# A fused SwiGLU feed-forward kernel: all loads issued by SyncE, ScalarE's table load first, x tile 1 transposed ahead of gate 0

## The chip, the cores and the metric

The kernel runs on one core of a Trainium2 chip. The time is the device time of one execution in microseconds; the figure compared is the median over runs. Five engines work side by side: TensorE (PE for matmuls, PEld for the load of their stationary operand), VectorE (DVE), ScalarE (ACT), GpSimd (POOL) and SyncE (SP). SyncE and ScalarE issue DMAs here, each on a queue of its own, and the same 16 DMA engines move the data of both.

## The reference

```python
def reference(x, w_gate, w_up, w_down):
    g = _silu(x @ w_gate)
    u = x @ w_up
    return (g * u) @ w_down
```

x is 1 x 2048 x 512, w_gate and w_up are 512 x 1376, w_down is 1376 x 512, all bf16.

## The kernel before

The 2048 tokens are worked in four chunks of 512. TensorE multiplies with 128 rows of the contraction at a time, so x must lie transposed: `xT_sb` holds it as 4 blocks of 128 features by 2048 tokens. For each chunk and each 128 columns of the weights there are a gate group and an up group, each of 4 matmuls into one of 8 PSUM banks; ScalarE applies silu to the gate bank, VectorE multiplies that by the up bank into `hT_sb`. The last 96 columns are worked apart (groups X and Y). Then comes the product with w_down, in strips, and the copies to `o_sb`, which SyncE (one of them ScalarE) stores.

The order on every queue is written out by hand, and semaphores tie the engines together. What concerns the change is the first chunk, where work starts before most of the input is there:

- Loads. ScalarE issues the first gate slab (128 columns, `load_gate(act, *slabs[0])`, line 121) and x tile 1 (line 122), then comes its table load for silu with a dummy activation (line 277). SyncE issues x tile 0, up slab 0, gate and up slabs of 1 and 2 column blocks, then two DMA transposes (`x0b`, `x0c`: tokens 256 to 383 and 384 to 511, line 95), the remaining gate and up slabs, the other chunks of x by DMA transpose, and w_down. A slab is named by its first block of 128 columns: `wg0`, `wu0`, `wg1`, `wu1`, `wg2`, `wu2`, `wg4`, `wu4` and so on.
- x tiles 0 and 1 (128 tokens each) are loaded as they lie (`load_xn`, line 115) and transposed by TensorE (`transposes`, line 367, four matmuls of 128 x 128 against an identity); VectorE and ScalarE copy the four results in turns from PSUM to `xT_sb` (lines 302 and 288).
- TensorE (`on_tensor`) starts with matmuls on constants (`warm`, line 358) that give no result, five of 512 columns and two of 128. Then, in this order: transposes of tile 0, two more such matmuls (`N_GAP`), gate group 0 on the first 128 tokens (four matmuls), transposes of tile 1, up group 0 on the first 128 tokens, both groups on tokens 128 to 255, the other six groups of the first eight banks on tokens 0 to 255, the first two groups on tokens 256 to 383 (they need `x0b`) and 384 to 511 (`x0c`), the other six on 256 to 511, and from there on whole groups of 512 tokens (line 326 throughout), the next of which needs `wg4`.

`need(name)` makes TensorE wait for a load, `after(engine, n)` for the n-th result of VectorE or ScalarE.

Of the kernel before, what the change touches and what calls it, by code (L numbers as in the profile page):

```python
# [14 lines left out]
def bass_standalone__swiglu_ffn__prompt_kernel(nc, x, w_gate, w_up, w_down, out):  # L15
    _, S, D = x.shape
    F = w_gate.shape[1]
    P = 128
# [32 lines left out]
    with ExitStack() as es:  # L51
# [33 lines left out]
        def load_sem(name):  # L85
            loads[name] = sem(f"s_{name}")
            return loads[name]
# [6 lines left out]
        def load_x(eng, name, t0, t1):  # L94
            eng.dma_start_transpose(
                xT_sb[:, :, t0:t1], xf[t0:t1, :]
            ).then_inc(load_sem(name), 16)

        def load_w(eng, name, src, base, f0, f1):
            eng.dma_start(  # L100
                w_sb[:, :, base + f0:base + f1],
                src[:, f0:f1].rearrange("(k p) f -> p k f", p=P),
            ).then_inc(load_sem(name), 16)

        slabs = [(0, 1), (1, 2), (2, 4), (4, 7), (7, NFT)]
        slab_of = {ft: a for a, b in slabs for ft in range(a, b)}

        def load_gate(eng, a, b):
            load_w(eng, f"wg{a}", w_gate, 0, a * P, min(b * P, F))

        def load_up(eng, a, b):
            load_w(eng, f"wu{a}", w_up, UPH, a * P, min(b * P, F - 32))

        def load_xn(eng, i):
            eng.dma_start(xn_sb[:, i, :], xf[i * P:(i + 1) * P, :]).then_inc(load_sem(f"xn{i}"), 16)
# [1 line left out]
        def out_rows(t):  # L117
            return of[t * P:(t + 1) * P, :]

        def loads_on_scalar(act):  # L120
            load_gate(act, *slabs[0])
            load_xn(act, 1)

        def loads_on_sync(sp):
            load_xn(sp, 0)
            load_up(sp, *slabs[0])
            for a, b in slabs[1:3]:
                load_gate(sp, a, b)
                load_up(sp, a, b)
            load_x(sp, "x0b", HT, HT + P)  # L130
            load_x(sp, "x0c", HT + P, SC)
            for a, b in slabs[3:]:
                load_gate(sp, a, b)
                load_up(sp, a, b)
            load_w(sp, "wut", w_up, F - (F - 32), F - 32, F)
            for c in range(1, NSC):
                load_x(sp, f"x{c}", c * SC, (c + 1) * SC)
            sp.dma_start(
                wd_sb[:, 0:NFF, :], w_down[0:NFF * P, :].rearrange("(k p) d -> p k d", p=P)
            ).then_inc(load_sem("wd"), 16)  # L140
            load_sem("wdt")
            for y0 in (0, 64):
                sp.dma_start(wd_sb[y0:y0 + 64, T01, :], w_down[NFF * P:F - SR, :]).then_inc(loads["wdt"], 16)
            for x0 in range(0, P, SR):
                sp.dma_start(wd_sb[x0:x0 + SR, T2, :], w_down[F - SR:F, :]).then_inc(loads["wdt"], 16)
            sp.dma_start(wd_sb[0:F_LAST, TAIL, :], w_down[NFF * P:F, :]).then_inc(load_sem("wdl"), 16)
# [7 lines left out]
        def add_group(kind, **what):  # L154
            g = dict(kind=kind, at=len(groups), bank=banks[len(groups) % NB], readers=[], **what)
            groups.append(g)
            return g
# [76 lines left out]
        for at, t in enumerate(tiles):  # L234
# [3 lines left out]
            for c0, c1 in parts:  # L238
                g = add_group("O", t=t, c0=c0, c1=c1)
                eng = "A" if at % 2 == 1 and c0 == 0 else "D"  # L240
                op = add_op(
                    eng, g, kind="copy", out=o_sb[ob][:, c0:c1], src=g["bank"][:, 0:c1 - c0],
# [8 lines left out]
        def ready(op):  # L251
            return op["ready"] if "ready" in op else (s_P, op["g"]["at"] + 1)

        def store_tiles(eng, own):
            for o, t, c0, c1, ob, copied, n in stores:
                if o == own:
                    eng.wait_ge(s_A if copied == "A" else s_D, n)
                    eng.dma_start(out_rows(t)[:, c0:c1], o_sb[ob][:, c0:c1]).then_inc(s_out[ob], 16)

        def on_sync(sp):  # L260
            loads_on_sync(sp)
            store_tiles(sp, "S")
            for i in range(NOS):
                sp.wait_ge(s_out[i], 16 * n_store[i])
# [8 lines left out]
            pool.tensor_copy(hl_sb[64:96, :], hx_sb[64:96, c, SC - P:SC]).then_inc(s_L, 1)  # L273

        def on_scalar(act):
            loads_on_scalar(act)
            act.activation(adummy[:, 0:4], zero_c, ACT.Silu)  # L277
            for op in act_ops:
                act.wait_ge(*ready(op))
                if op["kind"] == "silu":  # L280
                    if op["free"]:
                        act.wait_ge(s_D, op["free"])
                    fn = ACT.Silu
                else:
                    if op["stored"][1]:
                        act.wait_ge(*op["stored"])
                    fn = ACT.Copy
                act.activation(op["out"], op["src"], fn).then_inc(s_A, 1)  # L288
            store_tiles(act, "A")
# [15 lines left out]
        def on_tensor(pe):  # L305
# [25 lines left out]
            def gu_needs(g, n0, n1):  # L331
                c, ft = g["c"], g["ft"]
                if c > 0:
                    need(f"x{c}")
                if c == 0 and n1 > HT:
                    need("x0b")
                if c == 0 and n1 > HT + P:
                    need("x0c")
                need(("wg" if g["kind"] == "G" else "wu") + str(slab_of[ft]))

            def gu_step(g, dk, n0, n1):
                c = g["c"]
                col = (0 if g["kind"] == "G" else UPH) + g["ft"] * P
                if c == 0:
                    for i in range(n0 // P, min(n1 // P, NXN)):
                        after(*xt_ready[i, dk])
                ins = whole(g["bank"], dk, col, c, n0, n1)
                if n1 == SC and dk == KD - 1:
                    ins.then_inc(s_P, 1)

            def gu_matmuls(g, n0, n1):
                gu_needs(g, n0, n1)
                for dk in range(KD):
                    gu_step(g, dk, n0, n1)

            def warm(n, width):
                for i in range(n):
                    pe.matmul(banks[NB - 1][:, 0:width], lhsT=ones_w, rhs=ones_m[:, 0:width], start=True, stop=True)  # L358
# [5 lines left out]
            def transposes(i):  # L364
                need(f"xn{i}")
                for dk in range(KD):
                    pe.matmul(  # L367
                        tview(i, dk), lhsT=xn_sb[:, i, dk * P:(dk + 1) * P], rhs=ident[:, :],
                        start=True, stop=True, is_transpose=True,
                    ).then_inc(s_X, 1)  # L370

            first = groups[0:NB]
            transposes(0)
            warm(N_GAP, P)
            gu_matmuls(first[0], 0, P)
            transposes(1)
            gu_matmuls(first[1], 0, P)
            for dk in range(KD):
                for g in first[0:2]:
                    gu_step(g, dk, P, HT)  # L380
# [108 lines left out]
        on_sync(nc.sync)  # L489
        on_gpsimd(nc.gpsimd)  # L490
        on_scalar(nc.scalar)
        on_tensor(nc.tensor)
        on_vector(nc.vector)

# [27 lines left out]
```

## Time and profile before

| | us |
|---|---|
| median of 3 runs (lowest, highest) | 120.07 (120.05, 120.31) |
| the profiled execution | 120.41 |
| its span, first to last instruction | 119.1 |
| TensorE busy (matmul) | 116.5 |
| VectorE, ScalarE busy | 38.3, 35.2 |

The queues, from the page (packets, MB, share of the 16 engines' time over the span): q1 is SyncE's, q10 ScalarE's.

```profile
q1 hardware_dynamic: 16816, 8.33, 27.5%
q10 hardware_dynamic: 816, 0.36, 1.1%
```

A line of the timeline reads: start in us, length in us, engine, line of the kernel, operation, output<-inputs, shape, and how many like instructions in a row it merges; in brackets, the idle time of the engine before it and what ended it. SPq and ACTq are the issue of a DMA by SyncE and ScalarE, whose length is that of the issue and not of the transfer. The view of DMAs gives for each issue the KB and the us from its start to the landing of the last byte. A matmul's length in the trace includes its way through the array, which overlaps with the next one; the rate is seen from start to start.

### The profile page before, as it was taken

What the parts mean: (1) busy time and instruction counts of PE and PEld (TensorE: products, weight loads), DVE (VectorE), ACT (ScalarE), POOL (GpSimd) and SP (SyncE); (2) the same over time, 40 slices, a digit from 0 to 9 for tenths busy, and PEclk for the clock granted to TensorE, in tenths of its full rate; (3) what the DMA queues carried; (4) which work ended last, traced back from release to release, by engine and by line L of the source; (5) the groups of instructions that cost most, each with busy time, mean ns of one, the idle gap of its engine ahead of it and who ended that gap; (6) DMA issues with size and microseconds to landing.
All of it is one profiled execution on the core that took longest, in us unless ns stands there. A gap on an engine that the chain in (4) does not pass through costs nothing.

```text
span 119.1 us, 2344 instructions
## 1 busy us (share of the span) xinstructions
PE 116.5 (98%) x1019; PEld 60.6 (51%) x1019; DVE 38.3 (32%) x61; ACT 35.2 (30%) x62; POOL 1.0 (1%) x7
## 2 busy tenths in 40 slices
PE   7999999999999999999999999999999999999993
PEld 2899544444444444444444444444444445885452
DVE  0204633444334444334453344361000044003321
ACT  3406444262343272442353432430000033003021
POOL 1000000000000000000000000001000000000000
DMA  4999989991000000000000000000000017200612
GB/s 84 296 176 347 265 178 239 265 340 29 0 6 0 0 0 0 0 6 0 0 0 6 0 0 0 0 0 6 0 6 0 0 51 235 77 0 6 204 61 88
DMA packets 17642, 8.83 MB, mean 74 GB/s; under 512 B 10624, under 2 KB 17632, under 8 KB 17632
## 3 DMA queue, kind: packets, MB, share of 16 engines
q1 hardware_dynamic: 16816, 8.33, 27.5%
q10 hardware_dynamic: 816, 0.36, 1.1%
q8 instruction: 8, 0.13, 0.4%
q14 instruction: 2, 0.02, 0.1%
HBM read 4.75 MB, written 2.10 MB: 58 GB/s over the span
## 4 chain that ended last, share of the span: by engine, by line
PE 98%; DVE 0%; issue 0%
PE bank L326 62%; PE bank L444 25%; PE bank L483 7%; PE bank L358 2%; PE bank L406 2%; PE bank L367 1%; DVE o_sb L302 0%
## 5 line engine op out<-in xcount | busy, mean ns | idle before, releaser
L326 PE MATMUL bank<-xT_sb,w_sb 128*128 128x512 bf16 (+2 forms) x384 | 73.7, 356 | 0.0
L326 PEld LDWEIGHTS bank<-xT_sb,w_sb 128*128 128x128 bf16 x384 | 37.0, 100 | 36.3
L298 DVE TENSOR_TENSOR hT_sb<-sg_sb,bank 128x512 bf16<-128x512 f32 x40 | 27.5, 687 | 40.5 <-PE bank L326 39.6
L288 ACT ACTIVATE sg_sb<-bank 128x512 f32<-128x512 f32 x40 | 23.8, 596 | 40.9 <-PE bank L326 40.8
L444 PE MATMUL bank<-wd_sb,hT_sb 32*128 32x512 bf16 x496 | 29.0, 374 | 0.0
L444 PEld LDWEIGHTS bank<-wd_sb,hT_sb 32*128 32x128 bf16 x496 | 15.2, 93 | 11.6 <-issue 0.4
L302 DVE CAST o_sb<-bank 128x512 bf16<-128x512 f32 (+1 forms) x10 | 5.7, 595 | 31.1 <-PE bank L444 25.9
L288 ACT ACTIVATE o_sb<-bank 128x512 bf16<-128x512 f32 (+1 forms) x8 | 4.3, 582 | 33.6 <-PE bank L444 27.9
L483 PE MATMUL bank<-wd_sb,hT_sb 128*128 128x512 bf16 (+2 forms) x56 | 8.1, 304 | 0.0
L483 PEld LDWEIGHTS bank<-wd_sb,hT_sb 128*128 128x128 bf16 x56 | 4.2, 97 | 4.2 <-issue 0.4
L444 PE MATMUL bank<-wd_sb,hy_sb 32*128 32x512 bf16 (+1 forms) x32 | 5.0, 371 | 0.0
L298 DVE TENSOR_TENSOR hx_sb<-sgx_sb,bank 32x512 bf16<-32x512 f32 x4 | 2.8, 692 | 3.5 <-ACT sgx_sb L288 3.5
L288 ACT ACTIVATE sgx_sb<-bank 32x512 f32<-32x512 f32 x4 | 2.3, 587 | 4.5 <-PE bank L326 4.5
L358 PE MATMUL bank<-const-bfloat16-1.0 128*128 128x512 bf16 (+1 forms) x9 | 2.9, 486 | 0.8 <-PEq L507 0.8
L444 PE MATMUL bank<-wd_sb,hx_sb 32*128 32x512 bf16 (+1 forms) x16 | 3.0, 371 | 0.0
L288 ACT ACTIVATE sgy_sb<-bank 64x512 f32<-64x512 f32 x4 | 2.4, 590 | 0.1
L358 PEld LDWEIGHTS bank<-const-bfloat16-1.0 128*128 128x128 bf16 x9 | 1.1, 140 | 2.1 <-issue 2.1
L406 PE MATMUL bank<-xT_sb,w_sb 128*64 128x512 bf16 x16 | 1.9, 382 | 0.0
L444 PEld LDWEIGHTS bank<-wd_sb,hy_sb 32*128 32x128 bf16 x32 | 1.6, 93 | 0.6
L302 DVE COPY xT_sb<-bank 128x128 bf16<-128x128 bf16 x4 | 0.9, 224 | 3.0 <-PE bank L367 3.0
L277 ACT ACT_TABLE_LOAD x1 | 1.3, 1283 | 1.8 <-issue 1.8
L406 PEld LDWEIGHTS bank<-xT_sb,w_sb 128*64 128x64 bf16 x16 | 0.8, 109 | 1.0 <-DVE hT_sb L298 0.4
(16 smaller groups left out, 7.3 us busy)
## 6 DMA issues: line engine op xcount, KB each, us to landing
out_dram<-o_sb SPq DMA_DIRECT2D x15, 128.0 KB, 1.8
wd_sb<-in_w_down_dram SPq DMA_DIRECT2D x1, 1280.0 KB, 8.3
w_sb<-in_w_gate_dram SPq DMA_DIRECT2D x1, 480.0 KB, 5.5
w_sb<-in_w_up_dram SPq DMA_DIRECT2D x1, 448.0 KB, 7.5
w_sb<-in_w_gate_dram SPq DMA_DIRECT2D x1, 384.0 KB, 4.0
w_sb<-in_w_up_dram SPq DMA_DIRECT2D x1, 384.0 KB, 4.4
w_sb<-in_w_up_dram SPq DMA_DIRECT2D x2, 128.0 KB, 3.3
w_sb<-in_w_gate_dram SPq DMA_DIRECT2D x1, 256.0 KB, 3.7
```

What stands on the lines that cost most here:

```text
L277: act.activation(adummy[:, 0:4], zero_c, ACT.Silu)
L288: act.activation(op["out"], op["src"], fn).then_inc(s_A, 1)
L298: ins = dve.tensor_tensor(op["out"], op["a"], op["b"], ALU.mult)
L302: ins = dve.tensor_copy(op["out"], op["src"])
L326: return pe.matmul(bank[:, n0:n1], lhsT=w_sb[:, dk, col:col + P], rhs=xT_sb[:, dk, c * SC + n0:c * SC + n1], start=(dk == 0), stop=(dk == ...
L358: pe.matmul(banks[NB - 1][:, 0:width], lhsT=ones_w, rhs=ones_m[:, 0:width], start=True, stop=True)
L367: pe.matmul(tview(i, dk), lhsT=xn_sb[:, i, dk * P:(dk + 1) * P], rhs=ident[:, :], start=True, stop=True, is_transpose=True,).then_inc(s_X, 1)
L406: ins = pe.matmul(g["bank"][y0:y1, :], lhsT=w_sb[:, dk, YC0:YC0 + 64], rhs=xT_sb[:, dk, c * SC:(c + 1) * SC], start=(dk == 0), stop=(dk == ...
L444: ins = pe.matmul(g["bank"][:, 0:c1 - c0], lhsT=h, rhs=wd_sb[r0:r0 + SR, w, c0:c1], start=(start and fk == fks[0]), stop=(stop and fk == f ...
L483: ins = pe.matmul(g["bank"][:, 0:c1 - c0], lhsT=h, rhs=w, start=(last and fk == 0), stop=(fk == (NFF if last else NFF - 1)), skip_group_ch ...
```

## The change

SyncE takes over ScalarE's two loads: its order becomes x tile 0, gate 0, x tile 1, up 0, and from there as before. ScalarE's first instruction is then the table load. On TensorE the transposes of tile 1 come directly after the two filler matmuls, ahead of gate group 0, and the gate and up groups on the first 128 tokens follow one after the other.

```diff
-        def loads_on_scalar(act):
-            load_gate(act, *slabs[0])
-            load_xn(act, 1)
-
         def loads_on_sync(sp):
             load_xn(sp, 0)
+            load_gate(sp, *slabs[0])
+            load_xn(sp, 1)
             load_up(sp, *slabs[0])
             for a, b in slabs[1:3]:
                 load_gate(sp, a, b)
...
         def on_scalar(act):
-            loads_on_scalar(act)
             act.activation(adummy[:, 0:4], zero_c, ACT.Silu)
...
             transposes(0)
             warm(N_GAP, P)
-            gu_matmuls(first[0], 0, P)
             transposes(1)
-            gu_matmuls(first[1], 0, P)
+            for g in first[0:2]:
+                gu_matmuls(g, 0, P)
             for dk in range(KD):
                 for g in first[0:2]:
                     gu_step(g, dk, P, HT)
```

## The prediction

> **What bounds the kernel now.** I read the page's busy times and chain first, then the order of time of the first 16 us, then the landings, then the traffic in stretches.
>
> ```profile
> PE 116.5 (98%) x1019; PEld 60.6 (51%) x1019; DVE 38.3 (32%) x61; ACT 35.2 (30%) x62; POOL 1.0 (1%) x7
> ...
> PE 98%; DVE 0%; issue 0%
> ```
>
> TensorE is busy or in line for 98% of the span and the chain that ends last lies on it throughout. So a change to loads can move the time only through TensorE's few waits, all in the first 10 us, through the clock it starts with, or through the last stores. In order of time:
>
> ```profile
> 0.74 0.46 ACTq L100 DMA_DIRECT2D w_sb<-in_w_gate_dram  x1
> 0.74 0.40 SPq L115 DMA_DIRECT2D xn_sb<-in_x_dram  x1
> ...
> 1.19 0.42 SPq L100 DMA_DIRECT2D w_sb<-in_w_up_dram  x1
> 1.23 0.53 ACTq L115 DMA_DIRECT2D xn_sb<-in_x_dram  x1
> ...
> 1.79 1.28 ACT L277 ACT_TABLE_LOAD   x1 [1.79 <-issue]
> ...
> 3.26 0.35 PEld L367 LDWEIGHTS bank<-ident,xn_sb 128*128 128x128 bf16 x4 [0.25 <-issue]
> 3.29 0.58 PE L367 MATMUL bank<-ident,xn_sb 128*128 128x128 bf16 x4
> ...
> 3.67 0.42 PE L358 MATMUL bank<-const-bfloat16-1.0 128*128 128x128 bf16 x2
> 3.70 0.49 ACT L288 ACTIVATE xT_sb<-bank 128x128 bf16<-128x128 bf16 x2 [0.41 <-PE bank L367]
> ...
> 3.96 0.58 PE L326 MATMUL bank<-xT_sb,w_sb 128*128 128x128 bf16 x4
> ...
> 4.41 0.61 PE L367 MATMUL bank<-ident,xn_sb 128*128 128x128 bf16 x4
> ```
>
> The transposes of tile 0 start at 3.29 because x tile 0 lands then; the warm-up matmuls stopped at 3.07 (the last of them starts at 2.97 and passes on after 0.107), so 0.22 us are idle. After the two filler matmuls (done at 3.88) the gate matmuls wait 0.08 for the copies of tile 0; after them the transposes of tile 1 wait 0.05 for x tile 1. From 4.81 on no matmul waits. The landings, from each issue:
>
> ```profile
> w_sb<-in_w_gate_dram ACTq DMA_DIRECT2D x1, 128.0 KB, 2.9
> xn_sb<-in_x_dram SPq DMA_DIRECT2D x1, 128.0 KB, 2.4
> xn_sb<-in_x_dram ACTq DMA_DIRECT2D x1, 128.0 KB, 3.1
> ```
>
> So gate 0 lands at 3.59, x tile 0 at 3.15, x tile 1 at 4.36. The granted clock is 1.00 in every row, yet matmuls of one shape have two rates:
>
> ```profile
> 4.91 1.17 PE L326 MATMUL bank<-xT_sb,w_sb 128*128 128x128 bf16 x9
> ...
> 8.74 0.94 PE L326 MATMUL bank<-xT_sb,w_sb 128*128 128x128 bf16 x14
> ```
>
> Leaving out the last one's own duration (0.31 and 0.22 us, the rows of single instructions): (1.17-0.31)/8 = 0.107 us each early, (0.94-0.22)/13 = 0.056 later. The step comes at 5.95. Time lost before it therefore holds up work that could be made good at the double rate, if the step stays at 5.95: such a loss costs 1 - 0.056/0.107 = 0.48 of itself.
>
> ```profile
> 1.75:2.25 0.50, 0.50 (x3) 0.15 (x1) 0.00 (x0) 0.46 (x1) 0.00 (x0) 1.00 0.94 113
> 2.25:3.07 0.82, 0.82 (x4) 0.30 (x2) 0.00 (x0) 0.82 (x1) 0.00 (x0) 1.00 1.10 268
> 3.07:3.29 0.22, 0.21 (x2) 0.03 (x1) 0.00 (x0) 0.20 (x1) 0.00 (x0) 1.00 1.25 303
> 3.29:3.88 0.59, 0.59 (x6) 0.53 (x6) 0.29 (x2) 0.18 (x1) 0.00 (x0) 1.00 1.18 333
> ```
>
> (Stretch, its length, busy time and count of PE, PEld, DVE, ACT, POOL, then clock, DMA share, GB/s.) From 2.25 on the DMA engines are full: the loads wait for bandwidth, not for issue.
>
> **The change part by part.** *Table load first.* ScalarE loses two issues (0.74 to 1.76) and its table load (1.28) starts at about 0.74 instead of 1.79, its dummy activation ends near 2.2 instead of 3.29. Its first real work waits for TensorE until 3.70 with 0.41 idle before it, so this is worth nothing; left where it was, it would still be ready before the first copy.
>
> *x tile 0.* Same issue at 0.74, but gate 0 no longer shares the engines with it. Gain between 0 and 0.21 (TensorE is free at 3.07, so not sooner than 3.08). I take 0.07, near the lower end, since the slow part is the first half microsecond (113 GB/s), where little but x tile 0 was in flight. Transposes 0 start at 3.22, the fillers end 0.59 later as now: 3.81.
>
> *Order on SyncE.* Its issues follow at 0.45, 0.47, 0.54, 0.55, 0.55, 0.55 us (0.74, 1.19, 1.66, 2.20, 2.75, 3.30, 3.85). Two more 128 KB loads come before up 0: gate 0 moves to 1.19, x tile 1 to 1.66, and up 0 and all behind it go back by some 1.0 us.
>
> *Transposes 1 ahead of gate 0.* x tile 1 now comes when three loads of 131 kB, 393 kB in all, have been moved. The stretches give 57 + 220 + 67 = 343 kB by 3.29, and 50 kB more at 333 GB/s: 3.44. From bytes moved to landing: x tile 0's 131 kB are reached at 2.25 + 74/268 = 2.53 and landed at 3.15; the first six loads' 786 kB at 4.80 (251 kB in 3.88 to 4.81 at 270 GB/s added) and the sixth landed at 5.47. That is 0.62 and 0.67, so 4.09, and the weight load follows 0.04 later: 4.13. Bounds: 3.81 (no wait) and 1.66 + 3.13 + 0.04 = 4.83 (as long a way as now). Then twelve matmuls (transposes 1, gate, up) at 0.107, less 0.02 as the first after a wait come closer (4.41 to 4.81 for four): 4.13 + 1.26 = 5.39. Now this point is reached at 5.23. So +0.16, where +0.43 is paid for the gate matmuls no longer done during the wait, -0.27 comes from the earlier landing and the removed wait for copies. Gate 0 has landed long before; up 0 is needed at 4.13 + 0.83 = 4.96 and has four loads, 524 kB, moved by 3.84, landed by 4.5. The copies of tile 0 (done 0.9 us after their transposes start) hide behind the wait, those of tile 1 behind eight matmuls (0.86).
>
> In time: 0.16 x 0.48 = 0.08 if the clock's step stays at 5.95, 0.16 if it moves with the work; bounds -0.16 (no wait) and +0.86. By the Trainium skill (TensorE: Matmul & The Clock Gate, Part 1) the array's clock is released after a busy window of about 3.4 us that runs freely; the sum by this rule would be the 0.08, and no row here shows a window.
>
> *Later loads.* Gate 1, up 1, gate 2, up 2 land at 5.03, 5.47, 6.43, 7.21 and are needed at 6.06, 6.50, 6.93, 7.81. Issued 1.04 later they still find full engines (availability about 1.03 after issue, x tile 0's first packet: 1.77), so I take their landings as now, within 0.2: no wait. If the way from issue were as long as now, gate 2 would land at 7.47, 0.54 late. The DMA transposes: issued at 4.89 and 6.27 instead of 3.85 and 5.24, ways of 4.1 and 3.1 us. The first was queued behind up 2 and stays near 7.9 (needed at 8.68). The second lands between 8.34 (as now) and 6.27 + 3.10 = 9.37, needed at 9.13 + 0.08: wait of 0 to 0.2. I take 0, as its way also holds the first one's data. Gate 4 and up 4 land at 10.50 and 11.55, needed at 12.19 and 13.06: 1.0 later still fits. The rest has over 2 us.
>
> *Last stores.* ScalarE's store, now the first DMA on its queue, goes out at 117.18 and lands at 118.85; SyncE's lands last at 119.04. Cover 0.19; ScalarE's first issues took up to 0.53 where this one takes 0.36, so at most 0.17 is lost: nothing.
>
> Sum: +0.08 to +0.16, I take +0.1: span 119.08 to 119.18. The profiled execution took 120.41 with 1.33 around the span; the runs' median is 120.07, so the forecast is 120.17, by itself 119.95 to 120.30. No change is what lies within 0.2% (0.24 us), about what a measurement of this kernel can tell.
>
> **The rivals.** *A (slower): the later loads come late.* Place: gate 2 at 6.93 or the second DMA transpose at 9.13; decides once SyncE's extra 1.04 us isn't absorbed by the queue. Price: 0.54 - 0.16, or 0.2, on top of 0.1: 120.4 to 120.6. For: every later load is issued 1.0 later. Against: the full engines. *B (slower): the clock's step comes later.* Now it comes 2.66 after the 0.22 idle ends (3.29); counted so from the end of the wait before transposes 1 (4.13) it would come at 6.79: 0.84 x 0.48 = 0.40 on top of 0.08: 120.55. For: the new wait (0.3 us) is longer than the old. Against: the waits of 0.08 and 0.05 now didn't set it back. The Trainium skill (the same page, Part 4) says that transposes don't count as busy for the clock, which speaks for B too, since the new order puts both sets around the wait. *C (slower): x tile 1 takes the 3.13 us it takes now*, 4.83: +0.86 early, 0.41 to 0.86 in time: 120.5 to 120.9. Against: it has no weight load beside it. *D (faster): the first loads come so much sooner in one queue that TensorE never waits*: 3.08 + 18 x 0.107 = 5.01 instead of 5.23, and the step of the clock with it: 119.85, or lower with an earlier step. For: 0.35 us of waits to take. Against: the slow first half microsecond. *E: it does nothing that can be told*; inside the forecast's band.
>
> **How the numbers follow.** Forecast with E 0.46; A 0.17, B 0.10, C 0.10; D 0.17. A, B and C lie above +0.2%, D at or below -0.2%: faster 0.17, same 0.46, slower 0.37. Range 119.82 to 120.60: it holds the forecast, D and most of A and B.
>
> **What would show it.** Transposes 0 near 3.2, a wait of some 0.3 before transposes 1 near 4.1, the 128-column stage ending 0.1 to 0.2 later, the step of the clock still near 5.95, no wait at 6.93 or 9.13. A wait at these two would make A right, a later step B, x tile 1 landing after 4.6 C, no wait before transposes 1 D.

## The result and the profile after

The changed kernel takes 120.89 us (median of 7 runs, 120.58 to 121.30) against 120.19 (7 runs, 119.89 to 120.46) of the kernel before: ratio 1.0053, 95% interval 1.0031 to 1.0075. It is slower by about 0.7 us, beyond the 120.60 at which the stated range ended. The profiled execution took 121.30, the longest of the seven, with a span of 119.97, against 120.41 and 119.08; so its delays are larger than those of the median run. One run of e7 and two of e8 below, over 1.5% above the fastest of their kernel, are left out of the ratios but not of the medians (without them 122.28 and 122.03).

The chain that ended last, in order of time (start in us, length, what; the first pieces left out), and TensorE and its weight loads in the first 9 us:

```profile
3.23 0.51 SPq L100
3.73 0.04 issue
3.78 3.90 DMA w_sb<-in_w_gate_dram
7.67 0.05 issue
7.72 71.10 PE bank L323 x360
```

```profile
3.07 0.63 PE L364 MATMUL bank<-ident,xn_sb 128*128 128x128 bf16 x4
...
4.03 0.23 PEld L364 LDWEIGHTS bank<-ident,xn_sb 128*128 128x128 bf16 x4 [0.38 <-DMA xn_sb<-in_x_dram]
4.04 0.40 PE L364 MATMUL bank<-ident,xn_sb 128*128 128x128 bf16 x4
...
5.10 1.28 PE L323 MATMUL bank<-xT_sb,w_sb 128*128 128x128 bf16 x16 [0.45 <-DMA w_sb<-in_w_up_dram]
7.00 0.33 PEld L323 LDWEIGHTS bank<-xT_sb,w_sb 128*128 128x128 bf16 x4 [0.90 <-DMA w_sb<-in_w_up_dram]
...
7.71 0.77 PEld L323 LDWEIGHTS bank<-xT_sb,w_sb 128*128 128x128 bf16 x8 [0.38 <-DMA w_sb<-in_w_gate_dram]
...
8.64 3.41 PEld L323 LDWEIGHTS bank<-xT_sb,w_sb 128*128 128x128 bf16 x40 [0.15 <-DMA w_sb<-in_w_up_dram]
```

The chain, all TensorE before, now begins with SyncE's issues one after the other, ends in the landing of gate 2 (issued 3.78, landed 7.67) and only then goes over to TensorE. The timeline shows a wait for x tile 1 (4.04) and then four for weights: up 0 (5.10), up 1 (7.00), gate 2 (7.72), up 2 (8.64). From start to start, less the rate of the matmul before, these are 0.32, 0.61, 0.79, 0.27 and 0.04 us. Before, the group that needs gate 2 began at 6.93 with no wait for weights at all; it is now 0.79 later, the last wait adds 0.04, and the span has grown by 0.89 (0.06 of it is not accounted for here).

The bandwidth in three stretches (columns as in the prediction), first of the kernel before, then of the changed kernel:

```profile
3.25:4.25 1.00, 0.99 (x11) 0.82 (x10) 0.44 (x2) 0.53 (x3) 0.00 (x0) 1.00 1.19 307
4.25:5.25 1.00, 1.00 (x12) 0.94 (x11) 0.44 (x2) 0.41 (x2) 0.00 (x0) 1.00 1.19 269
5.25:6.25 1.00, 1.00 (x12) 0.99 (x11) 0.00 (x0) 0.08 (x1) 0.00 (x0) 1.00 1.09 325
```

```profile
3.25:4.25 1.00, 0.88 (x11) 0.62 (x9) 0.44 (x2) 0.49 (x2) 0.00 (x0) 1.00 0.82 195
4.25:5.25 1.00, 0.56 (x11) 0.38 (x9) 0.36 (x2) 0.45 (x2) 0.00 (x0) 1.00 1.14 250
5.25:6.25 1.00, 1.00 (x16) 0.83 (x14) 0.00 (x0) 0.00 (x0) 0.00 (x0) 1.00 0.82 191
```

A share below 1 says that some engines had nothing to do for part of the time. Bandwidth that the kernel before used is lost between 3.25 and 6.25, 265 kB in all (901 against 636), though every load up to gate 2 was issued by 4.29.

A load counts its semaphore up 16 times, and its landing is the last count. Of up 1's counts in the changed kernel 15 came by 5.95 and the last at 6.96. Of gate 2's, the first came at 6.45 (5.73 before), the eighth at 6.68 (6.00) and the last at 7.67 (6.43): half of its parts are some 0.7 later, and the rest of the 1.24 is parts that come later still. What holds single parts up stays open.

The clock. Four transposes from 4.04 on take 0.40 us in all where those from 3.07 took 0.63: the step to the double rate came between 3.7 and 4.04 here, not at 5.95. From 3.07 to the group that needs gate 2, TensorE is idle 1.99 us instead of 0.35, and busy 2.66 instead of 3.51, since the same matmuls ran at the higher rate. The early step thus makes good about half of the added waits in this profile; it can't move the end, which hangs on the landing of gate 2.

### The profile page after: what moved, and what is told of

It reads as the page before. It is cut to its first block, busy times and chain, and to the rows that moved or that the text cites. A ratio compares the mean times of both kernels' runs of the same rounds, so it can differ in the third digit from the quotient of the medians.

```text
span 120.0 us, 2344 instructions
## 1 busy us (share of the span) xinstructions
PE 116.1 (97%) x1019; PEld 59.6 (50%) x1019; DVE 38.3 (32%) x61; ACT 35.1 (29%) x62; POOL 1.0 (1%) x7
## 4 chain that ended last, share of the span: by engine, by line
PE 92%; DMA 3%; SPq 2%; issue 0%; DVE 0%
PE bank L323 59%; PE bank L441 25%; PE bank L480 7%; DMA w_sb<-in_w_gate_dram 3%; SPq L100 2%; PE bank L403 2%; SPq L115 1%; DVE o_sb L299 0%
## 5 line engine op out<-in xcount | busy, mean ns | idle before, releaser
L323 PEld LDWEIGHTS bank<-xT_sb,w_sb 128*128 128x128 bf16 x384 | 36.0, 98 | 38.1 <-DMA w_sb<-in_w_up_dram 1.7
L285 ACT ACTIVATE xT_sb<-bank 128x128 bf16<-128x128 bf16 x4 | 0.9, 276 | 1.6 <-PE bank L364 1.6
```

The costliest lines, as they stand in the source:

```text
L323: return pe.matmul(bank[:, n0:n1], lhsT=w_sb[:, dk, col:col + P], rhs=xT_sb[:, dk, c * SC + n0:c * SC + n1], start=(dk == 0), stop=(dk == ...
```

## The experiments

All against the kernel before, run beside them (medians 120.17 to 120.25), with the ratio's 95% interval. "Gate 2" gives issue and landing in that run's profile.

| run | time, us | ratio | gate 2 | span, us |
|---|---|---|---|---|
| the kernel before | 120.19 | 1 | 2.75, 6.43 | 119.08 |
| the changed kernel | 120.89 | 1.0053 (1.0031 to 1.0075) | 3.78, 7.67 | 119.97 |
| e1_pe_order | 120.19 | 1.0004 (0.9983 to 1.0025) | 2.75, 6.28 | 118.53 |
| e2_loads_only | 121.24 | 1.0079 (1.0053 to 1.0104) | 3.78, 7.46 | 119.71 |
| e3_before_again | 120.59 (one run) | | 2.75, 6.68 | 119.27 |
| e4_two_tiny | 121.06 | 1.0072 (1.0049 to 1.0094) | 3.71, 7.47 | 119.67 |
| e5_one_tiny | 120.69 | 1.0034 (1.0015 to 1.0052) | 3.23, 7.13 | 119.34 |
| e6_x_first | 120.74 | 1.0032 (1.0008 to 1.0056) | 2.75, 7.19 | 119.40 |
| e7_two_issuers | 122.38 | 1.0140 (1.0091 to 1.0189) | 2.68, 7.69 | 120.02 |
| e8_merged | 122.34 | 1.0146 (1.0112 to 1.0179) | (merged) | 121.00 |
| e9_table_first | 120.42 | 1.0017 (0.9995 to 1.0038) | 2.75, 6.58 | 118.79 |
| e10_late_issue | 120.87 | 1.0055 (1.0036 to 1.0074) | 3.40, 7.20 | 119.43 |
| e11_balanced | 121.03 | 1.0062 (1.0041 to 1.0084) | 2.20, 7.00 | 119.22 |

**e1_pe_order**, TensorE's part alone:

```diff
-            gu_matmuls(first[0], 0, P)
             transposes(1)
-            gu_matmuls(first[1], 0, P)
+            for g in first[0:2]:
+                gu_matmuls(g, 0, P)
```

> Loads as before, only TensorE's order changed (x tile 1 transposed ahead of gate 0). Theory 'issue' (the loss comes from one engine issuing all loads, so that up 0 and all behind it are issued 1.0 us later and arrive late): no loss of the size of the change; x tile 1 still lands near 4.36, transposes 1 start near 4.40, the first 128-token stage ends up to 0.43 late, in time -0.1 to +0.35, and no wait for a load after it. Rival 'order' (the new order itself costs the time, since gate 0 no longer fills the wait for x tile 1): +0.5 to +0.9, as the whole change.

No loss that can be told (1.0004). The wait before transposes 1 is there, and after it TensorE waits for weights only once, 0.03 for gate 2 (landed 6.28, its group starts at 6.33):

```profile
4.30 0.23 PEld L367 LDWEIGHTS bank<-ident,xn_sb 128*128 128x128 bf16 x4 [0.57 <-DMA xn_sb<-in_x_dram]
4.30 0.40 PE L367 MATMUL bank<-ident,xn_sb 128*128 128x128 bf16 x4 [0.31 <-DMA xn_sb<-in_x_dram]
```

(The timeline of that run.) The new order by itself isn't the cause.

**e2_loads_only**, the rest of the change with TensorE's order as before:

```diff
-            transposes(1)
-            for g in first[0:2]:
-                gu_matmuls(g, 0, P)
+            gu_matmuls(first[0], 0, P)
+            transposes(1)
+            gu_matmuls(first[1], 0, P)
```

(against the changed kernel)

> All loads on SyncE and the table load first as in the change, TensorE's order as before. Theory 'issue': +0.5 to +0.9 like the whole change, with waits for up 0 near 5.0, up 1 near 6.9, gate 2 near 7.7. Rival 'order': within 0.2 of the kernel before.

1.0079, as large as the whole change, with waits at 4.07 (gate 0), 5.15 (up 0), 6.31 (gate 1) and 7.51 (gate 2). Here the clock's step came at about 5.8, and gate 2 still sets the end. The loss is in the loads.

**e3_before_again**, the kernel before unchanged.

> The kernel before once more, for a second look at the clock: the step from 0.107 to 0.056 us for each 128-column matmul came at 5.95 there and between 3.7 and 4.0 in the changed kernel. If the step's place is chance, it comes elsewhere here, and the waits for loads before 10 us grow when it comes early; if the kernel sets it, it comes near 5.95 again.

The step came elsewhere, at about 6.5: the matmuls of 256 columns at 5.94 and 6.16 are still followed after 0.21, those from 6.57 on after 0.11. The other runs say the same: all start with the same warm-up matmuls at 0.77 or 0.78, and the last matmul that runs at the low rate, or in part at it, starts at 3.5 to 3.7 in e1, e4, e7, e9, e11 and the changed kernel, at 4.1 in e6, at 5.2 to 6.0 in e10, e5, e2 and the first profile of the kernel before, and at 6.4 to 6.5 in e8 and here. Early and late steps occur with the loads of before and with all loads on SyncE, in TensorE's old order and in the new one: nothing ties the place of the step to the change.

**e4_two_tiny**, two issues more on SyncE, next to no bytes:

```diff
             load_xn(sp, 0)
+            for i in range(2):
+                sp.dma_start(tiny[:, 4 * i:4 * i + 4], xf[0:P, 4 * i:4 * i + 4]).then_inc(s_tiny, 16)
             load_up(sp, *slabs[0])
```

(The lines that declare `tiny` and `s_tiny` are not shown.)

> The kernel before, with two loads of 1 KB in all each (128 rows of 8 bytes, into a scratch tile that nothing reads) issued by SyncE between x tile 0 and up 0: two issues more and next to no bytes. Theory 'issue': every load of SyncE from up 0 on is issued 0.9 us later and, as in the changed kernel, lands up to 1 us later: +0.4 to +0.8. Rival 'ring' (one queue moves less than two, whatever the issue): within 0.2 of the kernel before, as the two queues and their loads stay.

1.0072. ScalarE still issues its two loads, x tile 1 and gate 0 come in time, the same bytes are loaded: 0.94 us more ahead of up 0 in SyncE's queue cost as much as the change. Its timeline has the same waits (and one of 0.19 for up 1 at 6.25):

```profile
2.13 0.43 SPq L102 DMA_DIRECT2D w_sb<-in_w_up_dram  x1
...
4.93 1.00 PEld L330 LDWEIGHTS bank<-xT_sb,w_sb 128*128 128x128 bf16 x16 [0.49 <-DMA w_sb<-in_w_up_dram]
...
7.52 1.54 PEld L330 LDWEIGHTS bank<-xT_sb,w_sb 128*128 128x128 bf16 x15 [0.94 <-DMA w_sb<-in_w_gate_dram]
```

**e5_one_tiny**, the same with `range(1)`.

> The kernel before with one load of 1 KB in all issued by SyncE between x tile 0 and up 0 (one issue of about 0.46 us more, next to no bytes). Theory 'issue': up 2, which landed at 7.2 before and at 8.4 with two such loads, lands near 7.8, where TensorE first needs it at 7.8 when its clock rises late: between 0 and +0.4. A theory in which the small loads themselves clog the engines would have half of the two loads' loss, +0.43, or more.

+0.41 us, half of the two loads' loss, where both theories' bounds meet: it does not tell them apart. Up 2 landed at 8.02, later than the 7.8 expected.

**e10_late_issue**, which does: SyncE waits, and no DMA is added.

```diff
             load_xn(sp, 0)
+            sp.wait_ge(s_late, 1)
             load_up(sp, *slabs[0])
...
+            for i in range(4):
+                ins = pool.iota(late[:, i * P:(i + 1) * P], pattern=[[-1, P]], base=0, channel_multiplier=1)
+            ins.then_inc(s_late, 1)
```

(The lines that declare `late` and `s_late` are not shown.)

> The kernel before, with SyncE waiting between x tile 0 and up 0 for four iota instructions of GpSimd (0.23 us each, into a scratch tile that nothing reads): up 0 and all behind it are issued near 2.0 to 2.2 instead of 1.19, with no DMA added, moved or reordered. Theory 'issue': +0.5 to +0.9, up 2 lands near 8.2 to 8.5, as with two small loads. Rival 'more loads in one queue' (the number of loads in SyncE's queue, not their time of issue, costs it): within 0.2 of the kernel before.

Up 0 went out at 1.86, 0.67 late, a little sooner than expected, and up 2 landed at 8.10, just ahead of the 8.2 to 8.5 expected; 1.0055, in the range. A later issue by itself, with both queues and all loads as before, is enough for a loss as large as the change's. The engines run dry here as well, and the waits follow:

```profile
3.25:4.25 1.00, 1.00 (x12) 0.84 (x12) 0.44 (x2) 0.55 (x3) 0.00 (x0) 1.00 0.52 116
```

```profile
1.86 0.40 SPq L102 DMA_DIRECT2D w_sb<-in_w_up_dram  x1
...
5.17 1.77 PE L332 MATMUL bank<-xT_sb,w_sb 128*128 128x128 bf16 x20 [0.29 <-DMA w_sb<-in_w_up_dram]
...
7.25 1.95 PE L332 MATMUL bank<-xT_sb,w_sb 128*128 128x256 bf16 x16 [0.31 <-DMA w_sb<-in_w_gate_dram]
```

**e9_table_first**, the first part of the change alone:

```diff
-            loads_on_scalar(act)
             act.activation(adummy[:, 0:4], zero_c, ACT.Silu)
+            loads_on_scalar(act)
```

> The kernel before with ScalarE's dummy activation (and so its table load) ahead of its two loads in the program, nothing else: the first part of the change by itself. As ScalarE issued loads at 0.80 while its table load ran in the run with two issuers, both loads are issued within 0.1 of where they were: the same time, within 0.2 (theory 'issue'). A theory that the table load at the start costs something: +0.4 or more.

1.0017 with an interval that holds 1 (and reaches 1.0038): no effect that can be told. Its timeline shows that a table load ahead of loads doesn't hold up their issue:

```profile
0.74 1.28 ACT L276 ACT_TABLE_LOAD   x1 [0.74 <-PEq L507]
0.81 0.44 ACTq L100 DMA_DIRECT2D w_sb<-in_w_gate_dram  x1
```

**e7_two_issuers**, the changed kernel with up 0, 1 and 2 on ScalarE:

```diff
             load_xn(sp, 1)
-            load_up(sp, *slabs[0])
             for a, b in slabs[1:3]:
                 load_gate(sp, a, b)
-                load_up(sp, a, b)
...
             act.activation(adummy[:, 0:4], zero_c, ACT.Silu)
+            for a, b in slabs[0:3]:
+                load_up(act, a, b)
```

> The changed kernel, table load first and TensorE's order as in the change, but ScalarE issues up 0, up 1 and up 2 right after its table load and dummy activation (from about 2.25 on) while SyncE goes on with gate 1, gate 2 and the transposes. Theory 'issue': gate 1 is issued near 2.2, gate 2 near 2.7, the last of the three up loads near 3.4, so up 2 lands near 7.2 to 7.6 and the loss is mostly gone: -0.1 to +0.4 against the kernel before. Rival 'table load' or 'order' (something else in the change costs it): +0.5 to +0.9.

A miss in time: 1.0140. I had counted on ScalarE issuing after its table load; it issued at 0.80 while the table was loading, so the up loads went ahead of x tile 1 in the engines, which landed at 5.62, and transposes 1 waited:

```profile
0.80 1.55 ACTq L100 DMA_DIRECT2D w_sb<-in_w_up_dram  x3
...
5.67 0.40 PE L364 MATMUL bank<-ident,xn_sb 128*128 128x128 bf16 x4 [1.71 <-DMA xn_sb<-in_x_dram]
```

The profiled execution (121.35) is among the shortest of the six, which reach from 120.92 to 122.76; what the longer ones add is not shown. For the bytes it says what was asked: with two issuers up 2 landed at 6.74, and the packets moved by 6.5 are 1310 kB, as in the kernel before (1307), where the changed kernel has 1020.

**e8_merged**, the changed kernel with larger slabs, so two issues fewer:

```diff
-        slabs = [(0, 1), (1, 2), (2, 4), (4, 7), (7, NFT)]
+        slabs = [(0, 1), (1, 4), (4, 7), (7, NFT)]
```

(and the loops over `slabs` shifted by one)

> The changed kernel with the slabs of column blocks 1 and 2 to 3 merged: gate 1 to 3 is one load of 384 KB and up 1 to 3 another, so SyncE issues two loads fewer for the same bytes, all on one queue. Theory 'issue': these bytes are moved as soon as before, the up 1 to 3 load (issued near 3.2) lands at 7.0 to 7.5 instead of 8.4 to 8.6 as the last up load in the changed kernel; TensorE waits for it one group after it first needs gate 1, so the time itself is within 0.4 of the changed kernel's (+0.3 to +0.9 against before). Rival 'ring' (one queue moves less): it lands at 8.2 or later and the time is +1.3 or more.

A miss for the theory as I had put it: the merged up load, issued at 3.23, landed at 8.35, and the time is 1.0146. Fewer issues did not bring the bytes sooner; the stretches of this run:

```profile
3.25:4.25 1.00, 0.67 (x7) 0.40 (x4) 0.44 (x2) 0.49 (x2) 0.00 (x0) 1.00 0.78 193
4.25:5.25 1.00, 0.84 (x8) 0.77 (x8) 0.44 (x2) 0.41 (x2) 0.00 (x0) 1.00 0.88 199
5.25:6.25 1.00, 1.00 (x11) 0.84 (x10) 0.00 (x0) 0.08 (x1) 0.00 (x0) 1.00 0.93 295
```

The engines run dry here too, although the merged gate load was issued at 2.68: its first packets (768 bytes, told apart by their size) go at 4.2, and the rate reaches 295 GB/s only after 5.2. So fewer issues alone do not help. What fits this run, e4 and e10 alike is how long before the engines get to it a load was issued: here some 1.5 us until its first packets, 2.5 until that rate. In that time the queue was also still moving the loads ahead of it, so this is no pure lead time. The rival, that one queue moves less than two, would also fit this run. Against it stands the kernel before: ScalarE's two loads have landed by 4.36, and SyncE's queue alone moves 325 GB/s from 5.25 to 6.25; in the changed kernel it moves 323 from 6.25 to 7.25. What sets the lead time was not tried.

**e6_x_first**, two issuers, TensorE's new order, and ScalarE's loads swapped:

```diff
-            load_gate(act, *slabs[0])
             load_xn(act, 1)
+            load_gate(act, *slabs[0])
```

> Two issuers as before and TensorE's order of the change, but ScalarE issues x tile 1 ahead of gate 0. Theory 'issue': x tile 1 lands near 3.2 to 3.6, transposes 1 follow the two filler matmuls with a wait under 0.2, gate 0 (issued 1.23) lands near 4.1 and takes over as the wait; the loads from gate 1 on land as before: -0.3 to +0.1. Rival 'order' (nothing is to be had from x tile 1 first, since the byte stream decides): within 0.1.

A miss: 1.0032. In the profile x tile 0 landed at 3.62 instead of 3.15 and the weight loads from gate 1 to up 2 landed 0.7 to 1.0 later though issued as before. The counts tell how: of gate 1, up 1 and gate 2 the eighth came at 4.77, 5.34 and 6.07 (before: 4.71, 5.16, 6.00), the last only at 5.97, 6.43 and 7.19 (5.03, 5.47, 6.43). Half of the parts came nearly as before, and a few came late; why is open. So a load can also land late without having been issued late. The twelve runs spread from 119.99 to 121.16, so that profile isn't all of them.

**e11_balanced**, up 1 and up 2 moved to ScalarE, TensorE's order as in e1:

```diff
             load_xn(act, 1)
+            for a, b in slabs[1:3]:
+                load_up(act, a, b)
```

(and both left out on SyncE)

> TensorE's order of the change, and the loads split the other way: ScalarE issues gate 0, x tile 1, up 1, up 2, SyncE x tile 0, up 0, gate 1, gate 2 and then the transposes about 1.1 us sooner than before. Theory 'issue' (what matters is that loads are issued well before the engines get to them): no engine runs dry, up 2 lands at 6.7 to 7.2, -0.4 to +0.2 against the kernel before. Rival 'bytes' (the first 1.3 MB take until 6.5 to 6.7 whoever issues them, and splitting only mixes their order): gate 2 or the transposes land later than before, 0 to +0.5.

1.0062: the rival "bytes" holds. Gate 2, issued 0.55 sooner than before, landed 0.57 later (7.00), and gate 1 at 5.72 instead of 5.03, as loads that are needed later shared the engines with them (up 2's packets go from 4.95 to 7.00, gate 2's from 4.61 to 6.62). By 6.5 nearly the same bytes are moved (1277 kB) as before. The profiled execution is the shortest of the six (120.55, the median is 121.03) and its span is only 0.14 above that of before, so it shows the smaller part of the loss. Once the engines are full, as they are here, an earlier issue does not help. No version beat the kernel before.

**What the spans share.** In the nine traces in which gate 2 is the last real wait (the changed kernel, e1, e2, e4, e5, e6, e9, e10, e11) the span is the landing of gate 2 plus 112.19 to 112.30, wherever the clock's step came. In the two profiles of the kernel before it is 112.65 and 112.59: there TensorE, whose clock rose late, arrived at that group after gate 2 had landed.

The same loads issued at the same times do not land at the same time in every execution: gate 2 landed at 6.28, 6.43, 6.58 and 6.68 in the four traces with all loads issued as before, within 0.1 (e1, the kernel before, e9, e3), and at 7.46 and 7.67 in the two with all loads on SyncE (e2, the changed kernel). The eighth of its 16 counts parts the runs more clearly: 5.99 to 6.18 in the five in which SyncE issues as before (those four and e6), 6.68 to 7.16 in the five in which it issues up 0 and all behind it later (the changed kernel, e2, e4, e5, e10).

## Why the prediction was wrong

*The step that failed* is "Later loads": "Issued 1.04 later they still find full engines (availability about 1.03 after issue, x tile 0's first packet: 1.77), so I take their landings as now, within 0.2: no wait." The issue times were right (up 0 at 2.20, gate 2 at 3.78, up 2 at 4.33), the landings were not: up 0, gate 1, up 1, gate 2 and up 2 came 0.53, 0.48, 1.49, 1.24 and 1.39 later than before, of which 1.0 for up 1 is its one last part. Two things were wrong in it. The 1.03 was read from x tile 0, 128 pieces of 1 KB into an empty queue; gate 2's first packets in the changed kernel (512 bytes each) go 1.36 after its issue (5.14), a quarter of them only by 5.78, 2.0 after. And that the engines are full from 2.25 on was a fact of the old issue order, not of the bytes: they were full because each load had been issued well ahead. e10 shows it with nothing but time taken from SyncE (116 GB/s from 3.25 to 4.25 instead of 307), e4 with two all but empty loads. Why one issuer builds up no such lead is worked out, not tested: SyncE alone hands out its first six loads, 131 kB each, in 3.04 us (0.74 to 3.78), 259 GB/s, just under what the engines move (269 to 325). The pitch can't be all of it, since e8 hands out 917 kB by 3.23 (368 GB/s) and its engines run dry too.

The Trainium skill (DMA: Bandwidth & Descriptors, Issuing engines are not separate DMA queues) says that issuing on several engines only saves the issuing time, usually small beside the DMA. The first half is what these runs show, since two issuers do not beat the bandwidth (e7, e11); the second does not hold here: 0.5 us of issue stand against 0.40 to 0.49 for 131 kB at 325 to 269 GB/s, and an issue delay of 0.67 cost 0.55%.

*Rival A* named the mechanism and the place (gate 2), at 0.17 and priced too low: "the way from issue as long as now" gave gate 2 at 7.47 and a loss of 0.38 on top of the 0.1; it landed at 7.67 here, and at 7.46 in e2, whose span is 0.63 above that of before. A's objection, "the full engines", was the failed step itself.

*Transposes 0 and 1.* Foreseen at 3.22 and 4.13, they start at 3.07 and 4.04; x tile 0 landed at 2.91 without gate 0 beside it, a gain of 0.22 for which I had taken 0.07. x tile 1 landed at 3.99, foreseen at 4.09. This part of the sum holds, C (x tile 1 after 4.6) and D (no wait) are out, and in e1 the order alone costs nothing that can be told. The stage ends later all the same, as up 0, foreseen by 4.5, landed at 5.05.

*The clock.* I had left the step at 5.95 or let it move with the work, and kept B, a later step, as a rival. The profile has it between 3.7 and 4.04, and over all traces it moves by some 3 us with no tie to the change that could be found. The Trainium skill (TensorE: Matmul & The Clock Gate, Part 1) says that the window runs freely and that the number of slow matmuls differs from run to run; the traces agree with the second (3.5 to 6.5 for the last slow start), the window they do not show. The sum made against one execution thus stood on one draw: with an early step the kernel before needs its weights sooner too, as e9 shows, where gate 2 is waited for until 6.63.

*Table load and last stores* cost nothing that can be told, as foreseen: e9 for the first (1.0017, up to 1.0038); for the second, ScalarE's store goes out at 118.03 and lands 1.7 later, as before (117.18, 1.7), though it is the first on its queue.

*The transposed loads* (x0b, x0c) were foreseen near 7.9 and between 8.3 and 9.4; they landed at 9.15 and 9.57, but TensorE, late by then, needed them at 9.53 and 9.97 and did not wait.

## What to carry to other kernels

Full DMA engines are a property of the order of issue as much as of the bytes: before moving loads to one issuer, compare each load's lead over its use with the issuer's pitch (some 0.5 us for each load here), and test it by delaying the issuer alone. Take the way from issue to first bytes from a load of the same kind and place in the queue, not from the first one. Where the last wait ends on a load, as on gate 2 in nine traces here, the end of the kernel can be read off that load's landing. And read a landing from more than one execution, part by part: a single late part can hold a whole load.

## What the runs showed of the hardware that was not expected

A load of 128 rows by 4 pieces needs much longer from issue to its full rate than the first load suggested: 1.5 us to its first packets and 2.5 to 295 GB/s for the merged gate load of e8, behind four loads on the same queue, against 1.03 for x tile 0's first packet on an empty one.

A load lands in 16 parts, and a single one can come 1.0 after the fifteenth (up 1 in the changed kernel, 5.95 and 6.96).

ScalarE's sequencer issues DMAs while its table load runs: at 0.81, 0.07 after the load of 1.28 us began (e9).

TensorE's rate doubles at a point that differs by some 3 us between executions with the same start (last slow matmul at 3.5 to 6.5), and the granted clock in the rows is 1.00 throughout.
